# Three row blocks of q's fourth chunk made beside the late query blocks of attention

## The chip, the cores and the metric

The kernel runs on one core of a Trainium2 chip. The metric is the device time of one execution in microseconds; for the kernel before it is the median of three runs. The engines are TensorE (PE, with its weight loads PEld), VectorE (DVE), ScalarE (ACT), GpSimd (POOL) and SyncE (SP), which issues most of the DMAs.

## The reference

Two layers, each an attention block and a Fourier block, on x of 2048 rows and 640 columns:

```python
x = x + _A_ref(_layernorm(x), A_wqkv, A_wo)        # 32 heads of 20 columns
x = x + _B_ref(_layernorm(x), dft_seq_re, dft_seq_im, dft_hid_re, dft_hid_im)
x = x + _A_ref(_layernorm(x), A_wqkv, A_wo)
x = x + _B_ref(_layernorm(x), dft_seq_re, dft_seq_im, dft_hid_re, dft_hid_im)

# _A_ref: q, k, v = x @ wqkv; softmax(q k^T * 20**-0.5) v per head; result @ wo
# _B_ref: real part of DFT over rows of DFT over columns
```

## The kernel before, in words

**Tiling.** 32 heads go in 8 groups of four (`g`), 2048 queries in 4 query blocks of 512 (`qb`), 2048 keys in 16 key chunks of 128 (`kc`). A step `n` is one (`g`, `qb`, `kc`), so a layer's attention has 512 steps, 16 to a query block and 64 to a group (`s.steps`, L461). In each step PE makes four score products (`scores`, L518), two of them side by side on 62 rows each; ACT takes the exponential of two heads at a time (L521), two instructions per step; and PE multiplies the exponentials of an earlier step by v, four heads side by side on 32 columns each (`values`, L529; the trace has eight matmuls per step). Three PSUM buffers hold scores (`p0` to `p2`), seven SBUF buffers exponentials, and one PSUM bank the accumulator of a query block. At a query block's end `finish` divides and transposes on DVE and stores through POOL's queue (L536 to L550).

**The filler.** Only chunk 0 of q and of k (128 of the 640 columns) and half of v are made before attention starts. The rest is made beside it by the generator `work` (L381), piece by piece: k's and q's chunks 1 and 2, the other half of v (16 row tiles), then k's chunk 3, q's chunk 3 ("q's fourth chunk"), k's chunk 4, q's chunk 4. A chunk has four row blocks (`tb`) of 512 rows, each of 15 products of 128 x 128 by 512 columns (L99), cut into pieces of 8 and 7, or in the last two chunks of 5, 5 and 5 (L390). After a row block's last piece `keep` (L194) splits and squares the result on DVE and stores it through POOL's queue; two or four steps later `after` makes the row block's norms with one product (L212) and marks it as made. When the fourth row block of a chunk is done, `after` also splits the next chunk's weights on DVE (L84, L87) and fetches those of the chunk after that through SP's queue.

**What sets the order.** The order on each engine is written out by the loop `sweep` (L553). Per step it calls `begin`, which forces filler that the next heads need (`need`) and works out their softmax shift; loads the next query block's q; issues the two scores; calls `fill`, which issues at most one piece; and then the values that are owed. If a piece was issued, the values of that step are put off. Below step `THIN` = 236 they are made up for at once in the next step, from then on by a step with two steps' values (`calm`, `count = 2`).

`due` (L596) sets the pace of pieces by marks: 16 by step 44, 80 by step 236. From there on pieces come at the steps 2, 7 and 12 of a query block up to step 272 and at 2 and 10 later, until 104 are made.

**Deadlines.** A group's 80 columns of q come from one chunk or two. Group 4 has columns 320 to 399, so it is the first to read chunk 3. Group 6 (columns 480 to 559, `LATE`) is the first to read chunk 4, and is the one group for which only row block 0 of its second chunk has to be made when it starts: for each later query block it asks for the next row block at step 5, works out its own shift (DVE and POOL, L431 to L445; SP's DMA L447 at step 10) and loads q at step 10 (L496 to L499) in place of step 4.

Of the kernel before, what the change touches and what calls it, by code (L numbers as in the profile page):

```python
# [15 lines left out]
S, D, H, DH = 2048, 640, 32, 20  # L16
# [3 lines left out]
ND = D // 128  # L20
NT = S // 128
NB = S // 512
# [1 line left out]
GUARD = 30.0  # L24
NP = NT // 2
NQ = NT // 4
LATE = 512 // (4 * DH)
FIRST = (0, 1, 4, 5)
HD = D // 2
TOL = 2.0 ** -32  # L30
# [5 lines left out]
def mha_fnet_kernel(ctx, tc, x_in, wqk, wv, wo, seq, hid, nat_seq, nat_hid, out):  # L36
# [33 lines left out]
    def bank(tag, shape, name):  # L70
        return pools["pool"].tile(list(shape), F32, name=name, tag=tag)
# [30 lines left out]
    def pieces(blocks, n):  # L102

        todo = [f for b in blocks for f in b]
        for i in range(0, len(todo), n):
            for f in todo[i:i + n]:
                f()
            yield i + n < len(todo)
# [23 lines left out]
    class Qkv:  # L132
# [248 lines left out]
        def work(s):  # L381

            order = [ND + 1, 1, ND + 2, 2, ND + 3, 3, ND + 4, 4]
            w = {0: s.w1}

            def chunk(i):
                c = order[i]
                for tb in range(NB):
                    p = bank("fill", [128, 512], "pqk")
                    for more in pieces([s.product(p, w[i], tb, dc) for dc in range(ND)], 8 if i < 6 else 5):  # L390
                        if more:
                            yield True
                    sq = s.keep(p, c, tb, True, s.fill)

                    def after():
                        s.norms(bank("fill", [H, 512], "pn"), c, tb, sq)
                        s.made.add((c, tb))
                        if tb == NB - 1:
                            s.made.add(c)
                            if i + 1 < len(order):  # L400
                                w[i + 1] = s.weights(s.fill("w", [2, ND, 128], F32R, "wqk"), order[i + 1], True)
                            if i + 2 < len(order):
                                s.fetch(order[i + 2])
                    yield after

            for i in range(4):
                yield from chunk(i)
            for t in range(NT):
                p = bank("fill", [128, HD], "pv")
                for more in pieces([s.value(p, t, dc) for dc in range(ND)], 8):  # L410
                    if more:
                        yield True
                s.own(p, t, 1, True)
                yield None
            s.made.add("v")
            for i in range(4, 8):
                yield from chunk(i)

            s.silent = True
            r = s.bounds()  # L420
            ok = const.tile([128, 1], F32, name="ok", bufs=2)
            V.tensor_scalar(ok[:H], r[:H, 2:3], (GUARD / SCALE) ** 2, None, op0=OP.is_le)

            def after():
                p = bank("fill", [1, 1], "pok")
                PE.matmul(p, ok[:H], one[:H], start=True, stop=True)
                V.tensor_scalar(s.flag, p, float(H), None, op0=OP.is_equal)
            yield after
# [25 lines left out]
    class Attention:  # L454
# [98 lines left out]
        def sweep(s, shift, begin, fill):  # L553
            done = calm = 0
            for n, (g, qb, kc) in enumerate(s.steps):
                begin(n, g, qb, kc)
                last = qb == NB - 1
                if kc == (7 if last else 10 if g == LATE else 4) and not (last and g == H // 4 - 1):
                    s.qload(*((g, qb + 1) if not last else (g + 1, 0)), shift)
                if last and g + 1 < H // 4:  # L560
                    for f, j in {1: [(0, 0)], 9: [(0, 1)], 11: [(1, 0)]}.get(kc, []):
                        s.kload(g + 1, f, j)
                if qb == 0 and kc == 0 and g:
                    s.kload(g, 1, 1)
                s.scores(n, 0)
                s.scores(n, 1)

                more, owed = fill(n) and n >= 2 and n + 1 < len(s.steps), n - 1 - done  # L570
                if n < s.THIN:
                    if more and kc != 1:
                        continue
                    count = owed
                else:
                    if more and owed < 3:
                        calm = n + 2
                        continue
                    count = min(owed, 1)
                    if owed > 1 and (done + 1) % NT and n >= calm:  # L580
                        calm = n + 2
                        count = 2
                for _ in range(count):
                    s.values(done)
                    done += 1
            for n in range(done, len(s.steps)):
                s.values(n)

        def run(s, done, project, check):

            work, tasks, later = s.a.work(), s.a.vweights(1, s.a.fill, pause=[lambda: None] * 2), list(check)
            s.work, s.blocks, s.after, s.rest, s.more, s.landed = True, 0, None, 0, False, 0

            marks = ((0, 0), (44, 16), (s.THIN, 80))

            def due(n):  # L596
                for (n0, k0), (n1, k1) in zip(marks, marks[1:]):
                    if n < n1:
                        return s.blocks < k0 + (k1 - k0) * (n - n0) / (n1 - n0)
                return s.blocks < 80 or s.blocks >= 104 or (n - 1) % NT in ((2, 7, 12) if n < 272 else (2, 10))  # L600

            def block(n):
                try:
                    f = next(work)
                    s.blocks += 1
                    s.more = f is True
                    s.after = (n + (2 if n < s.THIN else 4), f) if f and not s.more else None
                    s.rest = s.after[0] + 2 if s.after else n
                except StopIteration:
                    s.work = False  # L610
                    tasks.extend(done())

            def fill(n):
                if s.after:
                    if n >= s.after[0]:
                        f, s.after = s.after[1], None
                        f()
                elif s.work and n >= s.rest and (s.more and n < s.THIN or due(n + 1)):
                    block(n)
                    s.rest = max(s.rest, n + 2)  # L620
                    return s.work and not s.a.silent

            def compare(n):


                if n < 8:
                    return
                for _ in range(2):
                    if not later or n < s.landed or (len(check) - len(later)) * 490 >= n * len(check):
                        break  # L630
                    task = later.pop(0)
                    if isinstance(task, tuple):
                        s.landed = n + 5
                        task = task[1]
                    task()

            def need(n, *keys):
                while not all(k in s.a.made for k in keys):
                    if s.after:
                        fill(s.after[0])  # L640
                    else:
                        block(n)

            def begin(n, g, qb, kc):


                if qb == NB - 1 and g + 1 < H // 4:
                    when, to = 0, g + 1
                    c0, c1 = to * 80 // 128, ((to + 1) * 80 - 1) // 128
                    keys = [c0, (c1, 0) if to == LATE else c1, ND + c0, ND + c1] + (["v"] if to >= 4 else [])  # L650
                else:
                    when, to, keys = 5, g, [(ND - 1, qb + 1)]
                if to != g or g == LATE and qb < NB - 1:
                    if kc == when:
                        need(n, *keys)
                        s.shift = s.a.bound(to, s.room)
                    if kc - when in (0, 3, 5):
                        next(s.shift)

                if tasks and n % 2 == 0 and n >= 16 and n % 64 < 54:  # L660
                    tasks.pop(0)()
                for f in project.early.get(n, []):
                    f()

            def between(n):
                more = fill(n)
                compare(n)
                return more

            s.sweep("b", begin, between)  # L670
            assert not s.work and not later and not tasks, (len(later), len(tasks))

# [856 lines left out]
```

## Time and profile before

| | us |
|---|---|
| median of 3 runs | 2523.99 (2523.82 to 2524.22) |
| the profiled execution | 2524.65 |
| its span in the trace | 2522.9 |
| attention of layer 1, first exponential to the end of the last | 87.58 to 1123.5 |
| attention of layer 2 | 1337.5 to 2374.6 |

The granted clock of TensorE was 0.999 over the span. In the page's busy digits, PE is at 9 tenths from the second slice to the last but one; ACT is at 8 and 9 in both attention stages and lower in the Fourier stages between and behind them. Filler, row sums of the weight check (L765, L769 on DVE) and the loads of the next stage's weights share the attention stages. Engines other than PE and ACT are busy for less than half of them.

A view of windows is a table by stretches of time: length, then the busy time of each engine with its instructions, the granted clock, the share of the DMA engines and GB/s. A timeline row has the start in us, the time it took, the engine, line, operation, tiles and count; idle time ahead of it, and who ended it, stand in brackets. A group's row has, behind the bar, busy us and mean ns, and behind the second bar idle time of the engine and its releasers.

### The profile page before, as it was taken

Reading aid. Unit: us, or ns where it says so; the run is one execution under the profiler, and the core shown is the slowest. Engines: PE = TensorE matmul, PEld = TensorE weight load, DVE = VectorE, ACT = ScalarE, POOL = GpSimd, SP = SyncE. Lnnn points to the kernel's source line nnn. Section 1 sums busy time; section 2 is a strip of 40 time slices with the busy share of each in tenths; the row PEclk is TensorE's granted clock in tenths of the full one; section 3 lists DMA queues with packets and bytes.
Section 4 is the critical chain, followed back from the end, with each engine's and each line's share of the span. In section 5 each row is a group of like instructions: output and inputs, shape, how many; then the busy total and the mean of one; then the engine's idle time right before and its main releaser. Section 6 shows DMA issues by size and latency. Waiting matters only on the chain. (4 is left out here: it accounts for less than half of the span.)

```text
span 2522.9 us, 43616 instructions
## 1 busy us (share of the span) xinstructions
PE 2492.9 (99%) x16350; PEld 1152.7 (46%) x16350; DVE 976.4 (39%) x2114; ACT 2134.2 (85%) x2430; POOL 520.5 (21%) x1022
## 2 busy tenths in 40 slices
PE   8999999999999999999999999999999999999998
PEld 7644444433333332249885444444433333322596
DVE  6245422243324233426753444223332323332275
ACT  5688899988999999985457888999899999999752
POOL 2012111122111112113321121111221111221133
PEclk9999999999999999999999999999999999999999
DMA  5224221222322223427553332222231222233365
GB/s 187 96 87 126 83 87 43 82 99 80 103 73 88 93 74 113 126 81 245 191 180 99 116 114 85 71 63 71 76 97 52 75 56 68 63 95 105 108 217 194
DMA packets 127024, 262.52 MB, mean 104 GB/s; under 512 B 28736, under 2 KB 53088, under 8 KB 126804
## 3 DMA queue, kind: packets, MB, share of 16 engines
q1 hardware_dynamic: 88212, 159.79, 19.5%
q0 software_dynamic: 38592, 99.85, 12.5%
q8 instruction: 132, 2.16, 0.4%
q14 instruction: 88, 0.72, 0.1%
HBM read 175.29 MB, written 84.21 MB: 103 GB/s over the span
## 5 line engine op out<-in xcount | busy, mean ns | idle before, releaser
L521 ACT ACTIVATE e<-psc 128x1024 f32<-128x1024 f32 x2048 | 1935.9, 1128 | 137.1 <-PE psc L518 103.7
L529 PE MATMUL acc<-e,v 128*32 128x512 f32 x8192 | 1058.6, 602 | 1.9 <-DVE of L536 1.8
L518 PE MATMUL psc<-stq,stk 62*128 62x512 f32 x4096 | 799.3, 458 | 1.3 <-ACT e L521 1.3
L518 PEld LDWEIGHTS psc<-stq,stk 62*128 62x128 f32 x4096 | 339.7, 184 | 808.6 <-ACT e L521 773.5
L529 PEld LDWEIGHTS acc<-e,v 128*32 128x32 f32 x8192 | 188.9, 108 | 370.0 <-issue 344.7
L550 POOL DMA_DIRECT2D o<-oh x256 | 131.7, 523 | 1009.1 <-DVE oh L545 1008.1
L99 PE MATMUL pqk<-xt,wqk 128*128 128x512 f32 x1200 | 318.6, 406 | 3.6 <-DVE wqk L84 1.5
L99 PEld LDWEIGHTS pqk<-xt,wqk 128*128 128x128 f32 x1200 | 213.5, 188 | 92.1 <-issue 41.3
L536 DVE STREAM_TRANSPOSE of<-acc 128x512 f32<-128x512 f32 x64 | 45.9, 717 | 537.1 <-PE acc L529 537.1
L84 DVE CAST hl<-pqk 128x512 fp32r<-128x512 f32 x64 | 44.2, 690 | 432.2 <-PE pqk L99 432.2
L99 PE MATMUL pv<-wv,xt 128*128 128x320 f32 x960 | 159.8, 317 | 0.0
L99 PEld LDWEIGHTS pv<-wv,xt 128*128 128x128 f32 x960 | 141.2, 188 | 25.5 <-issue 21.6
L550 POOL DMA_DIRECT2D o<-ot x256 | 129.0, 512 | 1.9 <-issue 0.7
L207 POOL DMA_DIRECT2D scrq<-hl x40 | 28.4, 709 | 350.9 <-DVE hl L87 219.3
L765 DVE TENSOR_REDUCE far<-cq 128x1 f32<-128x512 f32 (+5 forms) x169 | 98.5, 584 | 5.7
L92 PE MATMUL py<-wo,o 128*128 128x320 f32 x320 | 99.1, 310 | 1.4 <-DVE xr L947 1.4
L93 PE MATMUL py<-wo,o 128*128 128x320 f32 x320 | 98.6, 308 | 0.0
L94 PE MATMUL py<-wo,o 128*128 128x320 f32 x320 | 98.6, 308 | 0.0
L769 DVE TENSOR_TENSOR cq<-cq 128x512 f32<-128x512 f32 (+4 forms) x166 | 96.3, 580 | 2.9 <-DMA cq<-in_nat_seq_dram 2.7
L243 DVE COPY v<-pv 128x320 f32<-128x320 f32 x32 | 15.7, 490 | 204.1 <-PE pv L99 204.1
L207 POOL DMA_DIRECT2D scrk<-hl x40 | 27.9, 697 | 301.4 <-DVE hl L87 252.5
L213 DVE TENSOR_REDUCE top<-pn 32x1 f32<-32x512 f32 x80 | 53.5, 676 | 81.7 <-PE pn L212 81.7
(200 smaller groups left out, 1720.4 us busy)
## 6 DMA issues: line engine op xcount, KB each, us to landing
cq<-in_nat_seq_dram POOLq DMA_DIRECT2D x64, 512.0 KB, 5.5
scrq<-hl POOLq DMA_DIRECT2D x40, 512.0 KB, 3.2
scrk<-hl POOLq DMA_DIRECT2D x40, 512.0 KB, 3.3
stq<-scrq SPq DMA_DIRECT2D x256, 80.0 KB
stk<-scrk SPq DMA_DIRECT2D x128, 160.0 KB
o<-o SPq DMA_DIRECT2D x16, 1280.0 KB
stq<-scrq SPq DMA_DIRECT2D x256, 40.0 KB
stk<-scrk SPq DMA_DIRECT2D x128, 80.0 KB
```

The costliest lines, as they stand in the source:

```text
L92: PE.matmul(out_ap, ah, bh, start=start, stop=False)
L93: PE.matmul(out_ap, ah, bl, start=False, stop=False)
L94: PE.matmul(out_ap, al, bh, start=False, stop=stop)
L99: yield lambda i=i, j=j, k=k: PE.matmul(out_ap, a[i], b[j], start=dc == 0 and k == 0, stop=dc == ND - 1 and k == 2)
L207: G.dma_start(s.scr["qk"[k]][c * 128:(c + 1) * 128, :, tb * 512:(tb + 1) * 512], hl.bitcast(F32))
L213: V.tensor_reduce(s.top[:H, c // ND, c % ND, tb:tb + 1], p, op=OP.max, axis=AX.X)
L518: PE.matmul(p[:, i], s.k[g, kc // 8, j][r, kc % 8 * 128:(kc % 8 + 1) * 128], s.q[g, qb, j][r], start=True, stop=True)
L521: A.activation(e, p, AF.Exp, scale=SCALE)
L529: PE.matmul(s.acc[32 * j:32 * j + 32], s.a.v[kc][:, v0:v0 + 32], s.e[n, j // 2][:, j % 2], start=kc == 0, stop=kc == NT - 1, skip_group_ch ...
L550: G.dma_start(s.o[k, h * DH:(h + 1) * DH, qb * 512:(qb + 1) * 512], hl[k][32 * j:32 * j + DH])
L765: V.tensor_reduce(to, x, op=OP.max, axis=AX.X, apply_absolute_value=True)
L769: V.tensor_tensor(y, x, y, op=op)
```

## The change

`LATE` becomes a pair of groups, 4 and 6. Group 4 now starts when row block 0 of q's chunk 3 is made and asks for the others one by one, as group 6 does for chunk 4. Row blocks 1 to 3 of q's chunk 3 are cut into pieces of five, so that the projection has 107 pieces in place of 104. The mark at step 236 becomes 74 pieces (row block 0 of q's chunk 3 is piece 74), and from there on pieces stand at steps 2, 7 and 12 of each query block until 107 are made.

```diff
-LATE = 512 // (4 * DH)
+LATE = (256 // (4 * DH) + 1, 512 // (4 * DH))
...
-                    for more in pieces([s.product(p, w[i], tb, dc) for dc in range(ND)], 8 if i < 6 else 5):
+                    for more in pieces([s.product(p, w[i], tb, dc) for dc in range(ND)], 8 if (i, tb) < (5, 1) else 5):
...
-                if kc == (7 if last else 10 if g == LATE else 4) and not (last and g == H // 4 - 1):
+                if kc == (7 if last else 10 if g in LATE else 4) and not (last and g == H // 4 - 1):
...
-            marks = ((0, 0), (44, 16), (s.THIN, 80))
+            marks = ((0, 0), (44, 16), (s.THIN, 74))
...
-                return s.blocks < 80 or s.blocks >= 104 or (n - 1) % NT in ((2, 7, 12) if n < 272 else (2, 10))
+                return s.blocks < 74 or s.blocks >= 107 or (n - 1) % NT in (2, 7, 12)
...
-                    keys = [c0, (c1, 0) if to == LATE else c1, ND + c0, ND + c1] + (["v"] if to >= 4 else [])
+                    keys = [c0, (c1, 0) if to in LATE else c1, ND + c0, ND + c1] + (["v"] if to >= 4 else [])
                 else:
-                    when, to, keys = 5, g, [(ND - 1, qb + 1)]
-                if to != g or g == LATE and qb < NB - 1:
+                    when, to, keys = 5, g, [(((g + 1) * 80 - 1) // 128, qb + 1)]
+                if to != g or g in LATE and qb < NB - 1:
```

## The prediction

> **What bounds the kernel now.** I read the page first, for the shares and the costliest groups.
>
> ```profile
> PE 2492.9 (99%) x16350; PEld 1152.7 (46%) x16350; DVE 976.4 (39%) x2114; ACT 2134.2 (85%) x2430; POOL 520.5 (21%) x1022
> ...
> L521 ACT ACTIVATE e<-psc 128x1024 f32<-128x1024 f32 x2048 | 1935.9, 1128 | 137.1 <-PE psc L518 103.7
> ...
> L99 PE MATMUL pqk<-xt,wqk 128*128 128x512 f32 x1200 | 318.6, 406 | 3.6 <-DVE wqk L84 1.5
> ```
>
> A share of 99% says little, because PE is counted busy while it waits with a matmul in flight. The third row says more. L521 is the exponential of attention, two per step (one query block against one key chunk), 16 steps to a query block, 512 to a layer. ACT stood idle 137 us before it, 104 of them for the scores of PE. So somewhere PE is late for ACT. The view of windows, cut at the first exponential of chosen steps, tells where. Its columns are the stretch, its length, the busy time of PE, PEld, DVE, ACT and POOL, the clock and the DMA.
>
> ```profile
> 234.68:617.39 382.71, 380.85 (x2572) 159.88 (x2574) 136.42 (x273) 340.08 (x352) 67.45 (x120) 1.00 0.26 82
> 647.26:677.77 30.51, 30.51 (x212) 10.77 (x215) 9.48 (x17) 30.09 (x34) 4.97 (x9) 1.00 0.19 55
> 677.77:947.34 269.57, 269.57 (x1829) 90.86 (x1828) 92.42 (x203) 267.71 (x289) 52.98 (x96) 1.00 0.27 84
> 1484.80:1868.49 383.69, 381.26 (x2574) 159.89 (x2578) 130.73 (x261) 340.02 (x353) 66.72 (x120) 1.00 0.26 80
> 1928.85:2198.43 269.58, 269.58 (x1829) 90.83 (x1828) 77.45 (x186) 267.70 (x289) 51.18 (x96) 1.00 0.22 65
> ...
> 797.56:827.52 29.96, 29.96 (x207) 10.06 (x203) 10.24 (x18) 29.75 (x33) 6.08 (x11) 1.00 0.26 81
> ```
>
> The first row is steps 64 to 239 of layer 1, the second is steps 256 to 271, the third steps 272 to 415; the fourth and fifth are layer 2's, alike. Early, 11 query blocks take 34.8 us each and ACT works 340 of 383 us. Late, 9 take 29.95 us each and ACT is busy throughout. The groups of ACT in the first and third stretch, with their idle time, confirm it:
>
> ```profile
> L521 ACT ACTIVATE e<-psc 128x1024 f32<-128x1024 f32 x352 | 340.2, 1030 | 42.9 <-PE psc L518 32.7 <-PE acc L529 9.2 <-ACT e L521 0.2
> L521 ACT ACTIVATE e<-psc 128x1024 f32<-128x1024 f32 x289 | 268.8, 1070 | 1.9
> ```
>
> Early, ACT waits 42.9 us for PE: **PE bounds steps up to 236**, where each step also carries filler (projections of q, k, v in pieces). Late it waits 1.9 us: **ACT bounds the late steps**. Moving filler from the first to the second is a trade of PE time that counts for PE time that is partly covered.
>
> **The change, part by part.** (1) Pieces 75 to 80 of the filler, which are row blocks 1 to 3 of q's fourth chunk (45 products, six pieces of 8 or 7), leave the steps before 236 and become nine pieces of 5 after it. The order of instructions of the changed kernel shows that it does this: the rate up to step 236 is 58 pieces in 192 steps for 64, then pieces stand at steps 2, 7 and 12 of each query block through step 412, for two per query block before. The projection ends at nearly the same step (412 for 410).
>
> *What leaves the early steps.* One row block there, from the timeline of PE:
>
> ```profile
> 523.14 0.73 PE L518 MATMUL psc<-stq,stk 62*128 62x512 f32 x4
> ...
> 524.79 0.73 PE L518 MATMUL psc<-stq,stk 62*128 62x512 f32 x4
> 525.45 2.12 PE L99 MATMUL pqk<-xt,wqk 128*128 128x512 f32 x8
> 527.50 0.73 PE L518 MATMUL psc<-stq,stk 62*128 62x512 f32 x4
> ...
> 530.02 0.73 PE L518 MATMUL psc<-stq,stk 62*128 62x512 f32 x4
> 530.68 1.88 PE L99 MATMUL pqk<-xt,wqk 128*128 128x512 f32 x7
> 532.49 0.73 PE L518 MATMUL psc<-stq,stk 62*128 62x512 f32 x4
> ...
> 535.01 0.73 PE L518 MATMUL psc<-stq,stk 62*128 62x512 f32 x4
> ...
> 536.85 0.73 PE L518 MATMUL psc<-stq,stk 62*128 62x512 f32 x4
> ```
>
> Each step starts with four scores, so differences of these starts are step lengths: a plain step 1.65, the 8-piece 2.71, a step that catches up two steps of values 2.52, the 7-piece 2.47, another 2.52, the norm's step 1.84: 13.71 us for six steps. The plain step is 1.66 (657.92 to 659.58 below), six are 9.96. A row block thus costs 3.75 us of PE here, and three of them **11.3 us** per layer.
>
> Not all of it is won. With fewer pieces, stretches of three plain steps come up, and after three of them PE is ahead and waits for ACT. The nearest row is the step at 619.92, after three plain ones:
>
> ```profile
> 619.92 0.89 PE L518 MATMUL psc<-stq,stk 62*128 62x512 f32 x4
> ...
> 622.09 0.73 PE L518 MATMUL psc<-stq,stk 62*128 62x512 f32 x4
> ```
>
> 2.17 us, where the same step without a wait has 2.03 (below): 0.14 us. The order shows some ten such stretches among v's pieces: **1.4 us lost** (0 to 1.8).
>
> *What comes to the late steps.* A piece of five there:
>
> ```profile
> 657.92 0.73 PE L518 MATMUL psc<-stq,stk 62*128 62x512 f32 x4
> ...
> 659.58 0.73 PE L518 MATMUL psc<-stq,stk 62*128 62x512 f32 x4
> 660.24 1.44 PE L99 MATMUL pqk<-xt,wqk 128*128 128x512 f32 x5
> 661.61 0.73 PE L518 MATMUL psc<-stq,stk 62*128 62x512 f32 x4
> ...
> 663.27 0.73 PE L518 MATMUL psc<-stq,stk 62*128 62x512 f32 x4
> ...
> 665.78 0.73 PE L518 MATMUL psc<-stq,stk 62*128 62x512 f32 x4
> ```
>
> The piece's step is 2.03 and its catching up 2.51, so PE needs 10 x 1.66 + 3 x 2.03 + 3 x 2.51 + 0.18 for the norm = 30.40 us for a query block with three pieces, 0.44 over the 29.96 of one with two. The trace has one query block with three, 647.26:677.77 above: 30.51, that is 0.55 more. I take 0.5, between them. Nine query blocks (steps 272 to 415) get a third piece: **4.5 us** (4.0 to 5.0). The cover is PE's waiting for ACT in the two-piece query blocks. With it all gone, a piece costs 2.03 + 2.51 less two steps of 1.66, 1.22 us, and nine 11.0.
>
> (2) *The weights.* A chunk's weights are split on DVE when its predecessor ends. Once in the early steps this comes too late:
>
> ```profile
> 552.29 0.73 PE L518 MATMUL psc<-stq,stk 62*128 62x512 f32 x4
> ...
> 553.78 2.50 PE L99 MATMUL pqk<-xt,wqk 128*128 128x512 f32 x8 [0.75 <-DVE wqk L84]
> ...
> 556.21 0.73 PE L518 MATMUL psc<-stq,stk 62*128 62x512 f32 x4
> ```
>
> 3.92 us for a step of 2.71: 1.2 us. The new order puts three steps between split and use instead of two, so this stall shrinks (0 to 1.2 won, I take 0.6). In exchange the splits for the last two chunks stand two steps ahead of their use, at steps 288 and 352, by this row 0 to 1.2 us each; both come before the query block's own division on DVE, so I take 0.3 for the two. Net **0.3 won** (1.2 won to 2.4 lost).
>
> (3) *Head group 4.* Three more query blocks per layer have their own shift and load q at step 10 instead of 4. Group 6 already does so: SP, then PE.
>
> ```profile
> 901.29 0.25 SPq L447 DMA_DIRECT2D shiftb<-sh  x1
> ...
> 908.10 0.25 SPq L499 DMA_DIRECT2D stq<-shiftb  x1
> ```
> ```profile
> 916.31 0.93 PE L518 MATMUL psc<-stq,stk 62*128 62x512 f32 x4
> ```
>
> The shift waits on SP for DVE; behind it stand the twelve loads, which end their issue at 908.35, 7.96 us before the first scores that read them. PE's sequence runs through, and the third stretch above, which holds two of these turns, costs no more than others: **0**. The shift's power is worked out on POOL, and DVE waits for it with the filler's copies queued behind:
>
> ```profile
> L441 POOL TENSOR_TENSOR bound<-bound,powers 32x1 f32<-32x1 f32 x22 | 14.1, 641 | 96.4 <-DVE bound L435 96.3
> ```
>
> If DVE's idle time did not hide that, it would be 0.64 us for each of the three, 1.9 per layer.
>
> (4) DVE and POOL do the same copies and stores of a row block, later. DVE is idle for two thirds of the late steps, and three more of what eight row blocks already cause there stay under that: 0. Without this cover the norm waits for DVE, as once in the early steps, 0.3 us of the view of waits:
>
> ```profile
> PE pn L212 <- DVE sq L201: 0.3, 1, 0.3
> ```
>
> The tail after step 424 is unchanged.
>
> Sum per layer: -11.3 + 1.4 + 4.5 - 0.3 = -5.7 us; two layers -11.4 us. Against the profiled execution (2524.65 us, span 2522.9) this is 2513.25; against the median of 2523.99, 0.66 below it, **2512.6 us**.
>
> **The rivals.** *The third piece finds no cover.* If two pieces already use up all of PE's slack when every query block has three, each costs 1.22 us: 11.0 in place of 4.5, +6.5 x 2, 2525.6 us: no change. Against it stands the 30.51 of the one such query block; for it, that this one came after a lighter one and could draw on scores made ahead.
>
> *The early steps are not PE's.* If ACT or a chain through both set the early pace, nothing is saved and only the late cost stays: +4.5 x 2, 2533.0 us. It decides wherever the removed 11.3 us shrinks below 5.6. Against it stand the 42.9 us for which ACT waited on PE.
> The Trainium skill (Perfetto Trace Analysis, Identifying the Most-Contended Engine) judges TensorE's headroom by the busy share of its weight loads, not of its matmuls. By that the 159.88 of 382.71 us make PE far from bound and ACT, at 340, the contended engine, which would be this rival; the trace here disagrees, since ACT's idle time has PE as its releaser.
>
> *Late q loads (the slower side).* In group 4 the loads land after the first scores that need them, on three turns a layer, six in all. They must land 7.96 us after issue before it costs anything, and 11.4 / 6 = 1.9 us more before the kernel is slower. The trace has no landing of these loads; the nearest are
>
> ```profile
> cq<-in_nat_seq_dram POOLq DMA_DIRECT2D x64, 512.0 KB, 5.5
> scrq<-hl POOLq DMA_DIRECT2D x40, 512.0 KB, 3.2
> ```
>
> both shorter for larger transfers. At 3.8 us of waiting per turn: 2535.4 us.
>
> That the pieces do not move as said is excluded by the order of instructions.
>
> **How the numbers follow.** Forecast 0.84, no cover 0.07, early steps not PE's 0.05, late loads 0.04. The bounds of the unknown terms: at best 11.3 + 1.2 - 4.0 = 8.5 per layer, 2507; at worst 11.3 - 1.8 - 2.4 - 5.0 = 2.1, 2519.8. The range is 2507 to 2519.5; beyond it lie the three rivals. A measurement of this kernel tells about 0.2% (5 us) from no change, so faster means under 2518.9: 0.82, the forecast less 0.02 for its worst corner. Within 0.2%: that 0.02 and the first rival, 0.09. Slower: the other two, 0.09.
>
> **What would show it.** Right: query blocks of steps 272 to 415 near 30.45 us each, the steps up to 240 shorter by about 10 us in a layer, ACT idle some 10 us less there. Wrong: late query blocks near 31.2 (no cover), early steps as long as before, waits of L518 for a DMA at the turns of steps 272, 288 and 304, or waits for wqk at steps 290 and 354.

## The result and the profile after

| | before | after |
|---|---|---|
| median of 5 runs each, us | 2523.82 (2523.25 to 2524.22) | 2512.00 (2511.89 to 2512.25) |
| span of the profiled execution, us | 2522.9 | 2510.1 |
| attention of layer 1, from the first turn to the last, us | 997.48 | 991.64 |
| attention of layer 2, us | 998.67 | 991.94 |

The change takes 11.8 us off. The ratio is 0.9953, 95% interval 0.9942 to 0.9964. The forecast was 2512.6, the range 2507 to 2519.5. A turn is here the transposition of a query block's accumulator on DVE (L536); between the profiled executions attention lost 5.84 and 6.73 us, 12.6 of the 12.7 us that the span lost.

First the page of after: its engines and two of its groups.

```profile
PE 2479.9 (99%) x16350; PEld 1147.5 (46%) x16350; DVE 980.2 (39%) x2144; ACT 2133.1 (85%) x2430; POOL 524.1 (21%) x1028
...
L521 ACT ACTIVATE e<-psc 128x1024 f32<-128x1024 f32 x2048 | 1934.4, 1121 | 126.0 <-PE psc L518 94.1
L529 PE MATMUL acc<-e,v 128*32 128x512 f32 x8192 | 1057.9, 602 | 3.9 <-DVE of L536 3.8
```

PE has exactly as many matmuls as before (16350), and ACT as many instructions; what fell by 11.1 us is ACT's idle time ahead of the exponentials (137.1 before), 9.6 of it waiting for scores. The second group is the surprise: values now wait 3.8 us for DVE's transposition. In the page of before it was 1.8 us:

```profile
L529 PE MATMUL acc<-e,v 128*32 128x512 f32 x8192 | 1058.6, 602 | 1.9 <-DVE of L536 1.8
```

The view of windows of after shows where the time went, with the stretches of before cut at the same steps (layer 1: 64 to 239, 256 to 271, 272 to 415; layer 2: 64 to 239, 272 to 415; last, the query block of steps 336 to 351, as in the prediction's last row).

```profile
234.34:607.14 372.80, 371.01 (x2524) 151.85 (x2526) 127.20 (x259) 337.22 (x352) 65.29 (x117) 1.00 0.25 79
637.02:667.52 30.50, 30.50 (x212) 10.81 (x215) 10.21 (x22) 30.09 (x34) 5.54 (x10) 1.00 0.17 54
667.52:941.15 273.63, 273.63 (x1876) 96.60 (x1875) 100.92 (x220) 269.73 (x290) 56.13 (x101) 1.00 0.28 89
1478.58:1851.03 372.45, 370.65 (x2524) 151.71 (x2526) 121.79 (x246) 337.26 (x352) 64.52 (x117) 1.00 0.25 77
1911.41:2185.06 273.65, 273.65 (x1876) 96.52 (x1875) 85.96 (x203) 269.72 (x289) 54.29 (x101) 1.00 0.24 70
789.13:819.52 30.39, 30.39 (x212) 10.71 (x211) 10.25 (x18) 29.96 (x33) 6.15 (x11) 1.00 0.25 80
```

The early stretch fell from 382.71 to 372.80, 9.9 us. The late one rose from 269.57 to 273.63, 4.1 us, and 48 or 47 matmuls came into it (1829 to 1876) as they left the early one. The query block with three pieces that both kernels have stayed at 30.5. For layer 2 the row of before in the prediction begins 0.46 us ahead of step 64's first exponential; cut at the exponential it is

```profile
1485.26:1868.49 383.23, 380.80 (x2572) 159.76 (x2574) 130.53 (x260) 339.85 (x352) 66.72 (x120) 1.00 0.26 80
```

so layer 2 lost 10.8 early and rose by 4.1 late. The groups of ACT in after's first and third stretch say the same from the other side: early it waits 35.9 us (42.9 before), late 3.9 (1.9 before).

```profile
L521 ACT ACTIVATE e<-psc 128x1024 f32<-128x1024 f32 x352 | 337.3, 1036 | 35.9 <-PE psc L518 28.6 <-PE acc L529 6.5
L521 ACT ACTIVATE e<-psc 128x1024 f32<-128x1024 f32 x290 | 271.7, 1043 | 3.9
```

### The profile page after: what moved, and what is told of

It reads as the page before. It is cut to its first block, busy times and chain, and to the rows that moved or that the text cites. A ratio compares the mean times of both kernels' runs of the same rounds, so it can differ in the third digit from the quotient of the medians.

```text
span 2510.1 us, 43669 instructions
## 1 busy us (share of the span) xinstructions
PE 2479.9 (99%) x16350; PEld 1147.5 (46%) x16350; DVE 980.2 (39%) x2144; ACT 2133.1 (85%) x2430; POOL 524.1 (21%) x1028
## 3 DMA queue, kind: packets, MB, share of 16 engines
q0 software_dynamic: 38592, 99.85, 12.6%
## 5 line engine op out<-in xcount | busy, mean ns | idle before, releaser
L518 PE MATMUL psc<-stq,stk 62*128 62x512 f32 x4096 | 786.2, 455 | 1.3 <-ACT e L521 1.3
L518 PEld LDWEIGHTS psc<-stq,stk 62*128 62x128 f32 x4096 | 335.5, 184 | 792.3 <-ACT e L521 762.6
L536 DVE STREAM_TRANSPOSE of<-acc 128x512 f32<-128x512 f32 x64 | 45.8, 716 | 349.9 <-PE acc L529 349.3
```

The source lines that it names most:

```text
L518: PE.matmul(p[:, i], s.k[g, kc // 8, j][r, kc % 8 * 128:(kc % 8 + 1) * 128], s.q[g, qb, j][r], start=True, stop=True)
```

## The experiments

**The theory** (trade): 11.3 us of PE's time per layer leave steps in which every microsecond of PE lengthens the kernel and go to steps in which PE waits for ACT, so that only a part of it shows. **The rivals**: the gain is the vanished stalls and the new order, not the work (order); it is the cut into smaller pieces (cutting); the late pieces cost their whole 1.22 us and the gain comes from elsewhere (no cover), or they are free; the late loads of group 4 cost or hide something. Two more theories came up as experiments failed: that the late slack needs **evenly spaced** pieces, and that a row block which ends at a turn delays the **hand-over** of the accumulator. Each run is compared with the kernel before on the same chip, whose medians were 2523.67 to 2523.89.

**e1_left_out: the late work taken away**, from the changed kernel. One product of fifteen is left of each of the three row blocks.

```diff
-                    for more in pieces([s.product(p, w[i], tb, dc) for dc in range(ND)], 8 if (i, tb) < (5, 1) else 5):
+                    blocks = [s.product(p, w[i], tb, dc) for dc in range(ND)]
+                    if i == 5 and tb:
+                        blocks = [[lambda: PE.matmul(p, w[i][:, 0, 0], s.xt[tb, 0][0], start=True, stop=True)]]
+                    for more in pieces(blocks, 8 if (i, tb) < (5, 1) else 5):
...
-                return s.blocks < 74 or s.blocks >= 107 or (n - 1) % NT in (2, 7, 12)
+                return s.blocks < 74 or s.blocks >= 101 or (n - 1) % NT in ((2, 7, 12) if n < 320 else (2, 10))
```

> The changed kernel with row blocks 1 to 3 of q's fourth chunk left out but for one product of fifteen each (that part of q is not computed); splits, stores and norms stay, the pace of the late pieces is three per query block up to step 320 and two from there on. It shows the early saving almost alone. Trade theory (11.3 us of TensorE time per layer leave the early steps, some 1.4 us come back as waits, each third late piece costs 0.45): early -9.9 per layer as in the changed kernel, three query blocks with a third piece +1.3, step 240 to 255 some 0.4 shorter: -9.0 x 2 against the kernel before, 2505.8 us (2504.5 to 2507.5), about 6 us under the changed kernel. Stall theory (the gain is the 1.2 us wait for weights at step 212 that is gone, and the slower pace): as fast as the changed kernel less what the late pieces cost, and the early steps as long as there. If late pieces were free: 2512 again, less 0.8.

Measured: 2505.94 us (2505.60 to 2506.42). Its windows of the early and the late stretch of layer 1 (like those of e2_made_twice, e3_uncut and e10_bunched below, they are cut at the first scores of a step, 0.6 to 1.1 us ahead of its first exponential):

```profile
233.49:605.95 372.46, 370.26 (x2518) 151.30 (x2514) 128.67 (x261) 336.62 (x353) 65.77 (x119) 1.00 0.26 81
666.26:937.05 270.79, 270.79 (x1846) 92.82 (x1843) 95.39 (x214) 268.27 (x289) 54.61 (x99) 1.00 0.28 86
```

The early stretch is as in after; the late one is 2.8 us shorter. So the late pieces do cost: 6.1 us in both layers together. "Free" falls.

**e2_made_twice: the late work added, nothing taken away**, from the kernel before. The three row blocks are made early as before; behind them, among the late steps, come as many products again, in pieces of five, with the next chunk's weights and a result that nobody reads.

```diff
+                for tb in range(1, NB) if i == 5 else ():
+                    p = bank("fill", [128, 512], "pqk")
+                    for more in pieces([s.product(p, w[6], tb, dc) for dc in range(ND)], 5):
+                        yield True if more else None
...
-                return s.blocks < 80 or s.blocks >= 104 or (n - 1) % NT in ((2, 7, 12) if n < 272 else (2, 10))
+                return s.blocks < 80 or s.blocks >= 113 or (n - 1) % NT in (2, 7, 12)
```

> The kernel before with the cost of the late pieces alone: everything is made early as before, and nine further pieces of five products, whose result nobody reads, are put among the late steps at the changed kernel's pace (no copies, stores or norms for them). Trade theory: nine third pieces at 0.45 less the three norms that are missing (0.18 each), 3.5 to 4.1 us per layer: 2531.3 us (2530 to 2532.5). No cover: nine at 1.22 us, 11 us per layer: 2546. Late pieces free: 2523.8.

Measured: 2532.57 us (2532.43 to 2532.71), 8.9 above before and 0.07 above the upper end of what was expected. Early and late stretch:

```profile
233.54:616.02 382.48, 380.62 (x2571) 159.76 (x2568) 136.73 (x274) 339.63 (x353) 67.22 (x121) 1.00 0.26 82
676.84:950.01 273.17, 273.17 (x1869) 95.84 (x1865) 94.11 (x201) 269.51 (x289) 54.27 (x98) 1.00 0.27 86
```

The early stretch is that of before (382.71), the late one nearly that of after: the two halves of the trade stand each by itself. Nine pieces of five per layer would have cost 22 us in both layers without cover. "No cover" falls.

**e6_pace: the new places alone**, from the kernel before: pieces of 8 and 7 and of 5 as before, but at 2, 7 and 12 throughout.

```diff
-                return s.blocks < 80 or s.blocks >= 104 or (n - 1) % NT in ((2, 7, 12) if n < 272 else (2, 10))
+                return s.blocks < 80 or s.blocks >= 104 or (n - 1) % NT in (2, 7, 12)
```

> The kernel before with the late pace alone: its 24 late pieces come at three per query block instead of two and are done at about step 360; nothing leaves the early steps. Trade theory: the query blocks with three pieces cost 30.41 instead of 29.96, and those that become empty 29.25 instead of 29.96. Of nine query blocks (steps 272 to 415) six get a third piece, +2.7, and three become empty, -2.1: +0.6 per layer, 2525.0 us (2523.5 to 2526). If the three-per-query-block pace were itself the gain: under 2520.

Measured: 2526.51 us (2526.07 to 2526.89), 2.8 us above before and 0.5 above the range expected: a miss in size. Attention rose by 0.68 and 1.27 us. The denser pace is a small loss by itself, so the new places of the late pieces are not the source of the gain. What is left of "order" is the stall on the weights, which is worth 1.2 us per layer (below), a fifth of the gain.

**e5_group5: one more group that asks late**, from the changed kernel: group 5 too works out its own shifts and loads q at step 10.

```diff
-LATE = (256 // (4 * DH) + 1, 512 // (4 * DH))
+LATE = (256 // (4 * DH) + 1, 256 // (4 * DH) + 2, 512 // (4 * DH))
```

> The changed kernel with the late shift and the late loads of q (step 10 instead of 4) for head group 5 as well, which needs neither: three more such turns per layer, six in all, and no filler moved. Trade theory: the loads have 8 us to spare and the shift is hidden, 0: 2512.0 us (2511.6 to 2512.5). Late-load theory: the three turns of group 4 already cost something, and so would these, 1 us of waiting for scores on each of them making 6 us: 2515 or more.

Measured: 2512.42 us (2511.89 to 2513.05), the same as after. Late loads cost nothing measurable, in group 5 as in group 4.

**e3_uncut: the change without the cut**, pieces of 8 and 7 for the three row blocks.

```diff
-                    for more in pieces([s.product(p, w[i], tb, dc) for dc in range(ND)], 8 if (i, tb) < (5, 1) else 5):
+                    for more in pieces([s.product(p, w[i], tb, dc) for dc in range(ND)], 8 if i < 6 else 5):
...
-                return s.blocks < 74 or s.blocks >= 107 or (n - 1) % NT in (2, 7, 12)
+                return s.blocks < 74 or s.blocks >= 104 or (n - 1) % NT in (2, 7, 12)
```

> The changed kernel with row blocks 1 to 3 of q's fourth chunk in pieces of 8 and 7 instead of three of five, moved out of the early steps all the same. Trade theory: TensorE's products are what counts, not how they are cut; the query blocks from step 240 to 303 then sum to 120.6 us by the step lengths (2.71, 2.47, 2.03, 2.51, 1.66) for 121.2 in the changed kernel, with 0.7 more in the query block before them: 2512.2 us (2511 to 2514). If the finer cut carries the gain: towards 2520 or more. If a piece of 8 starves ScalarE beyond the sum of steps, by the 0.7 us gaps seen behind such pieces early: six pieces, up to 4 us per layer, 2520.

Measured: 2516.75 us (2516.52 to 2518.16), a miss: 4.75 us, two fifths of the gain, are gone. The windows of the query blocks at steps 240 and 256:

```profile
607.06:638.19 31.13, 31.13 (x212) 10.80 (x208) 11.08 (x21) 29.98 (x33) 6.26 (x11) 1.00 0.38 111
638.19:669.31 31.12, 31.12 (x212) 10.97 (x208) 11.98 (x25) 29.97 (x33) 5.37 (x10) 1.00 0.20 60
```

Two pieces of 8 and 7 are as many products as three of 5, and the steps add up to 30.3 us, yet the query block takes 31.1. Between two pieces there are more plain steps (steps without a piece) in a row. That gave the theory of even spacing: the three score buffers hold the scores of one and a half steps, so PE gets only so far ahead of ACT. In a plain step it gains some 0.17 us on ACT (1.66 us against 1.83); after about three of them the buffers are full, and what it could save beyond that it waits away.

**e10_bunched: the same pieces, unevenly spaced**, from the changed kernel, made to test that.

```diff
-                return s.blocks < 74 or s.blocks >= 107 or (n - 1) % NT in (2, 7, 12)
+                return s.blocks < 74 or s.blocks >= 107 or (n - 1) % NT in (2, 5, 8)
```

> The changed kernel with the late pieces at steps 2, 5 and 8 of a query block instead of 2, 7 and 12: the same work, bunched. Sum theory as predicted (a query block with three pieces costs TensorE's 30.40 us wherever they stand): 2512 to 2513. Evenness theory (three score buffers let TensorE run ahead by three plain steps, then each further one waits 0.15 us for ScalarE; the uncut pieces cost 31.13 us a query block by it, where their steps sum to 30.3): seven plain steps in a row, four or five of them waiting, 31.1 us a query block and eleven query blocks a layer: +7 to 8 per layer, 2527 us (2522 to 2530), and all of the gain is lost.

Measured: 2527.92 us (2527.77 to 2528.13), 15.9 above after and 4.0 above before. Windows of steps 272 to 415 and of one query block of them:

```profile
667.85:947.69 279.84, 279.84 (x1877) 97.81 (x1874) 101.77 (x224) 271.25 (x289) 56.40 (x101) 1.00 0.28 89
698.96:730.06 31.10, 31.10 (x214) 10.86 (x210) 10.86 (x25) 30.23 (x33) 7.38 (x13) 1.00 0.31 94
```

No matmul more, 6.2 us longer; 31.10 per query block for after's 30.40. The timeline of PE at the starts of six steps in the long plain run shows how:

```profile
724.90 0.73 PE L518 MATMUL psc<-stq,stk 62*128 62x512 f32 x4
...
726.56 0.73 PE L518 MATMUL psc<-stq,stk 62*128 62x512 f32 x4
...
728.22 0.86 PE L518 MATMUL psc<-stq,stk 62*128 62x512 f32 x4
...
730.00 0.98 PE L518 MATMUL psc<-stq,stk 62*128 62x512 f32 x4
...
731.91 0.84 PE L518 MATMUL psc<-stq,stk 62*128 62x512 f32 x4
...
733.67 0.91 PE L518 MATMUL psc<-stq,stk 62*128 62x512 f32 x4
```

The step lengths are 1.66, 1.66, 1.78, 1.91, 1.76. Ahead of these stand one more plain step and the norm's step. So after three plain steps the four scores take 0.84 to 0.98 us instead of 0.73, and the steps lengthen to about ACT's pace, 1.83 us (a query block without filler takes 29.33 us, turn to turn). What ends the wait is an exponential, which frees a score buffer for the next weight load of the scores:

```profile
730.41 0.26 PEld L518 LDWEIGHTS psc<-stq,stk 62*128 62x128 f32 x2 [0.23 <-ACT e L521]
```

What PE waits here it lacks at the next piece. The cover is whole only where a piece comes after at most three plain steps.

**e4_one_block: a third of the change.** Only row block 3 moves.

```diff
-                    for more in pieces([s.product(p, w[i], tb, dc) for dc in range(ND)], 8 if (i, tb) < (5, 1) else 5):
+                    for more in pieces([s.product(p, w[i], tb, dc) for dc in range(ND)], 8 if (i, tb) < (5, 3) else 5):
...
-            marks = ((0, 0), (44, 16), (s.THIN, 74))
+            marks = ((0, 0), (44, 16), (s.THIN, 78))
...
-                return s.blocks < 74 or s.blocks >= 107 or (n - 1) % NT in (2, 7, 12)
+                return s.blocks < 78 or s.blocks >= 105 or (n - 1) % NT in ((2, 7, 12) if n < 320 else (2, 10))
```

> A third of the dose: only row block 3 of q's fourth chunk is moved behind step 236 (mark 78 pieces, three per query block up to step 320, two from there on). Trade theory: early -3.75 per layer and some 0.5 of waits back, three third pieces +1.35, so -1.9 per layer, 2520.0 us (2518.5 to 2522); in proportion to the full change. Stall theory: all of the gain or none of it, according to whether the weights' split stands clear of its use: 2512 to 2514, or 2523.8.

Measured: 2524.68 us (2523.04 to 2526.13), a miss: no gain at all. The profiled execution, at 2523.04 us, was its fastest; attention in it is 997.82 us in each layer, 0.5 us less than before for both together, where 3.8 were expected. PE's work moved as priced, 3.76 us less early per layer, and steps 242 to 417 rose by 1.3 us. The view of PE's waits, steps 98 to 241 of layer 1 and of layer 2, has the reason:

```profile
PE acc L529 <- DVE of L536: 3.1, 5, 2.4
...
PE acc L529 <- DVE of L536: 2.1, 5, 1.1
```

Its columns are total, count and the longest. One wait of 2.4 us; the timeline around it, DVE and PE:

```profile
581.60 1.88 PE L99 MATMUL pqk<-xt,wqk 128*128 128x512 f32 x7
...
583.52 0.69 DVE L84 CAST hl<-pqk 128x512 fp32r<-128x512 f32 x1 [8.21 <-PE pqk L99]
...
584.24 0.69 DVE L87 TENSOR_TENSOR hl<-pqk,hl 128x512 fp32r<-128x512 f32 x1
...
584.85 0.68 DVE L201 TENSOR_TENSOR sq<-hl 128x512 bf16<-128x512 f32 x1
...
585.45 0.68 DVE L769 TENSOR_TENSOR cq<-cq 128x512 f32<-128x512 f32 x1
586.16 0.69 DVE L765 TENSOR_REDUCE far<-cq 128x1 f32<-128x512 f32 x1
586.77 0.70 DVE L536 STREAM_TRANSPOSE of<-acc 128x512 f32<-128x512 f32 x1
...
587.53 1.06 PE L529 MATMUL acc<-e,v 128*32 128x512 f32 x8 [2.39 <-DVE of L536]
```

The last piece of a row block falls into step 225, just at the turn. DVE stands idle 8.2 us, then does the row block's three operations and two of the weight check ahead of the transposition that frees the accumulator, and PE waits. So the work moved as meant, but another piece came into a bad slot by it.

**e8_one_block_clear: no piece at any turn**, from e4_one_block.

```diff
-                elif s.work and n >= s.rest and (s.more and n < s.THIN or due(n + 1)):
+                elif s.work and n >= s.rest and (n >= s.THIN or n % NT not in (0, 1)) and (s.more and n < s.THIN or due(n + 1)):
```

> The run that moved one row block gained nothing, and its trace shows TensorE waiting 2.4 us at step 226 of layer 1 and 1.1 us in layer 2 for the transpose of the accumulator, which stood on VectorE behind a row block's three copies and a weight check; the row block had ended at step 1 of the query block. This is that kernel with no piece issued at steps 0 and 1 of a query block below step 236. Hand-over theory (a row block that ends at the turn delays the accumulator's transpose, and the trade itself is as priced): the wait goes and the third of the gain appears, 2520.0 us (2518.5 to 2521.5). If the trade is not in proportion (one block simply brings nothing): 2523.5 to 2525.

Measured: 2524.92 us (2523.38 to 2526.48), a miss. The wait at step 226 went, but the edit shifts pieces in every query block. By the waits of PE in steps 28 to 62 of layer 1, one new wait took its place,

```profile
PE pn L212 <- DVE sq L201: 2.1, 1, 2.1
```

a norm forced at once where pieces now crowd, with the same 2.1 us in layer 2; some 5 us of PE's work came from ahead of step 98 to behind it; and the span ended 9.2 us after the last operation of DVE, for 6.8 in e4_one_block. It moved too much to decide.

**e12_one_block_225: that one slot alone**, from e4_one_block.

```diff
-                elif s.work and n >= s.rest and (s.more and n < s.THIN or due(n + 1)):
+                elif s.work and n >= s.rest and n not in (224, 225) and (s.more and n < s.THIN or due(n + 1)):
```

> The run that moved one row block, with one edit: no piece at steps 224 and 225, so the row block that ended at step 225 ends at step 226, behind the turn, and all pieces from step 236 on stand as they were. (Keeping steps 0 and 1 clear everywhere took that wait away, but pushed pieces together at step 48, where a forced norm waited 2.4 us for VectorE, and the time did not fall.) Hand-over theory: the waits of 2.4 us in layer 1 and 1.1 us in layer 2 go, up to 0.3 us of the shorter kind stays in each, and the trade of one row block, -3.76 early and +1.33 late per layer, comes out: 3 us under the run without the edit, 2521.6 us (2520.5 to 2522.5). If one row block simply brings nothing: 2524.7.

Measured: 2521.50 us (2520.42 to 2522.73), as expected, 3.2 us under e4_one_block. The waits of PE over the same steps, layer 1 and layer 2:

```profile
PE acc L529 <- DVE of L536: 0.7, 4, 0.2
...
PE acc L529 <- DVE of L536: 1.0, 4, 0.5
```

Turn to turn, the query block of steps 208 to 223 fell from 40.26 to 36.23 us in layer 1, and the piece that was barred lengthened the next one from 31.96 to 33.76. The hand-over theory holds: the time came back with this one slot. Against before, the gain of a third of the work is 2.3 us in the medians, and 3.8 us, 1.9 per layer, in the attention of the profiled executions.

**e9_checks_clear: the weight check off the turns**, from the changed kernel, which has a small wait of this kind:

```diff
-                if n < 8:
+                if n < 8 or n % NT in (0, 1):
```

> The changed kernel with no weight checks issued on VectorE at steps 0 and 1 of a query block; they are made up for in the steps behind. Its trace has one long wait for the accumulator's transpose, 0.76 us at step 226 of layer 1, with a check of 1.4 us between the row block's copies and the transpose. Hand-over theory: that wait goes, 0.5 us of 0.76, and nothing else moves: 2511.5 us (2510.8 to 2512.3).

Measured: **2511.24 us** (2511.08 to 2511.78), ratio to before 0.9949, interval 0.9935 to 0.9963. It is the fastest version, 0.8 us under the change, and within what was expected. The timeline of after at step 226, and then that of this kernel:

```profile
576.71 0.69 DVE L769 TENSOR_TENSOR cq<-cq 128x512 f32<-128x512 f32 x1
577.43 0.69 DVE L765 TENSOR_REDUCE far<-cq 128x1 f32<-128x512 f32 x1
578.03 0.70 DVE L536 STREAM_TRANSPOSE of<-acc 128x512 f32<-128x512 f32 x1
...
578.79 1.06 PE L529 MATMUL acc<-e,v 128*32 128x512 f32 x8 [0.56 <-DVE of L536]
```
```profile
576.25 0.68 DVE L201 TENSOR_TENSOR sq<-hl 128x512 bf16<-128x512 f32 x1
...
577.46 0.72 DVE L536 STREAM_TRANSPOSE of<-acc 128x512 f32<-128x512 f32 x1 [0.53 <-PE acc L529]
...
578.23 1.07 PE L529 MATMUL acc<-e,v 128*32 128x512 f32 x8
```

Without the two check operations DVE waits for PE there, not PE for DVE. Attention fell by 0.6 and 1.4 us. The 0.6 is this wait. Layer 2 has none at step 226; there the gain comes from two waits of 0.56 us at steps 34 and 82, which went as well. The kernel before has these two too, so this part is an improvement of its own and takes nothing back that the change cost. The profiled spans differ by less than 0.2 us, because 1.0 us more passed behind DVE's last operation (last section) and 0.7 us more between the two attention stages.

**e7_aligned: the pieces of steps 96 to 236 at 2, 7 and 12 of their query blocks too**, from the changed kernel, so that no row block ends at a turn.

```diff
-                        return s.blocks < k0 + (k1 - k0) * (n - n0) / (n1 - n0)
+                        return s.blocks < k0 + (k1 - k0) * (n - n0) / (n1 - n0) + (3 if n >= 96 else 0) and (n < 96 or (n - 1) % NT in (2, 7, 12))
```

> The changed kernel with the pieces of the early steps from 96 on put at fixed steps of the query block (2, 7, 12 and two steps behind each) instead of by the mark alone. The changed kernel's trace has two residual waits of TensorE early: 0.24 us at step 2 of a query block when its first values wait for the transpose of the accumulator, and 0.12 to 0.19 us after three plain steps. A piece at step 2 puts the values off and the first wait goes; long plain stretches between pieces bring more of the second. By counts of steps some 2.4 us per layer less and up to 1.5 us more: 2510.2 us (2508 to 2512.5). If the position of pieces does not matter early: 2512.0.

Measured: 2512.02 us (2511.72 to 2513.13), no difference. The waits for the transposition are gone from those steps, but attention is 990.75 and 992.07 us for 991.64 and 991.94. By step lengths, the fixed places leave stretches of more than three plain steps, and PE waits at their ends, at steps 153 to 156, 174 to 178, 202 to 204, 218 to 220 and 234 to 236: 0.11 to 0.24 us a step, some 2.9 us per layer. That took the place of the waits that went. The expected 1.8 us were not there.

**e11_v_cut: v's row tiles in pieces of five products in place of eight**, from the changed kernel, to get rid of its stretches of three plain steps.

```diff
-                for more in pieces([s.value(p, t, dc) for dc in range(ND)], 8):
+                for more in pieces([s.value(p, t, dc) for dc in range(ND)], 5):
...
-            marks = ((0, 0), (44, 16), (s.THIN, 74))
+            marks = ((0, 0), (44, 16), (96, 32), (203, 80), (s.THIN, 90))
...
-                return s.blocks < 74 or s.blocks >= 107 or (n - 1) % NT in (2, 7, 12)
+                return s.blocks < 90 or s.blocks >= 123 or (n - 1) % NT in (2, 7, 12)
```

> An attempt at a faster kernel: the changed kernel with v's pieces too cut into five products (three per row tile instead of 8 and 7), spread evenly over steps 96 to 203. By the evenness theory the waits of 0.12 to 0.19 us behind three plain steps go, ten per layer, and TensorE's sum stays: some 1.4 us per layer less the waits that new positions bring, 2510.5 us (2509 to 2512.5). If the early steps are at TensorE's sum in any case: 2512.0.

Measured: 2515.88 us (2515.24 to 2517.30), a miss, 3.9 above after. Attention rose by 0.55 and 0.97 us; a row of PE's waits in steps 27 to 246 of layer 1 names the new one,

```profile
PE acc L529 <- DVE of L536: 2.0, 5, 0.9
```

with its longest at step 114, where more and smaller pieces bring DVE's copies to a turn. Of the rest, 2.4 us lie behind DVE's last operation, at the end of the program (last section).

## Why the prediction was right, point by point

To compare the terms, steps without a wait were priced from the timelines: four scores 0.80 us, eight values 0.86, a product of q or k 0.239, of v 0.155, the norm 0.18. What a stretch is longer than the sum of its steps is PE's waiting. Per layer, layer 1 / layer 2:

| | before | after |
|---|---|---|
| steps 98 to 241, sum of work | 306.4 | 295.1 |
| steps 98 to 241, waiting | 2.0 / 1.9 | 3.5 / 2.4 |
| steps 242 to 417, sum of work | 321.2 | 332.5 |
| steps 242 to 417, waiting (layer 1) | 8.8 | 1.7 |

**The mechanism held.** 11.3 us of PE's work went from the first stretch to the second, where 7.1 us of waiting disappeared under it. e1_left_out and e2_made_twice show the two halves apart.

- *What leaves the early steps*, 11.3 forecast: 11.29.
- *Waits after three plain steps*, 1.4 lost: ten waits of 0.12 to 0.19 us, 1.45 in layer 1, and some 1.2 in layer 2. After's timeline at one of them, step 130, from its scores to the next step's, is 2.19 us for 2.04 without a wait:

```profile
375.25 0.89 PE L518 MATMUL psc<-stq,stk 62*128 62x512 f32 x4
376.07 1.43 PE L99 MATMUL pv<-wv,xt 128*128 128x320 f32 x8
377.44 0.73 PE L518 MATMUL psc<-stq,stk 62*128 62x512 f32 x4
```

- *What comes late*, 4.5 (4.0 to 5.0): 4.06 and 4.07, nine times 0.45. The prediction chose 0.5 between the sum of steps (30.40) and the one measured query block (30.51). The sum was the better of the two: nine query blocks in 273.63 us are 30.40 each, the length of PE's work, so PE sets it and waits no more. The 30.51 of the block of steps 256 to 271 was no better row: by step lengths PE still waits 0.35 us at its step 256 and 0.19 at 258, in both kernels, since no piece stands between steps 247 and 258.
- *The weights*, 0.3 won: 1.2 won. The views of waits of the early steps, before and then after:

```profile
PE pqk L99 <- DVE wqk L84: 0.8, 1, 0.8
...
PE acc L529 <- DVE of L536: 0.4, 2, 0.2
...
```
```profile
PE acc L529 <- DVE of L536: 1.4, 6, 0.6
...
```

  The stall at step 212 is gone whole, and no wait stands at steps 290 or 354: the two steps ahead of these uses were enough.
- *Group 4's loads*, 0: 0, by e5_group5.
- **Missed:** the last view's first row. With the pieces of the early steps at other places, values wait longer for the transposition, 1.4 us for 0.4 (layer 2: 1.4 for 0.9). One of the new waits, 0.56 us in layer 1 alone, stands at step 226, where a row block ends near the turn; e9_checks_clear takes it away. Three more in each layer are of 0.17 or 0.18 us, at steps 146, 194 and 210, where no piece puts off the first values of a query block; e7_aligned, with a piece at that place, has none of them. The prediction costed DVE's copies only for the norm, not for the transposition queued behind them.
- **ACT's idle time**, a sign that was to show it: "some 10 us less" in the steps up to 240. It fell by 7.0 us in layer 1 (42.9 to 35.9), while the stretch became 9.9 us shorter; the rest is 2.9 us by which ACT's busy time in it fell.

So the sum was -5.7 per layer and came out at -5.8 and -6.7. The errors partly offset each other: late pieces 0.4 cheaper, weights 0.9 better, hand-over 0.5 to 1.0 worse. That the forecast came within 0.6 us of the median is therefore in part luck; the direction and the size of the two large terms are not.

Two things the prediction had without naming them. Its late price holds only because the pieces stand five steps apart (e3_uncut, e10_bunched); the same 11.3 us bunched would have made the kernel slower than before. And its early price holds only where no turn is hit: e4_one_block moved a third of the work and won nothing. The Trainium skill (Perfetto Trace Analysis, Optimization Strategy) says that a gap which repeats on the engine that should be saturated can mean too few buffers for the next tile. The waits of 0.12 to 0.19 us after each third plain step, with three score buffers, agree with that; no run here changed the number of buffers.

Of the rivals, "no cover" would have had late query blocks near 31.2 and they took 30.40; "early steps not PE's" would have left 382.7 us and it was 372.8, which also speaks against the headroom by weight loads that the prediction set beside it; "late loads" has no wait of L518 for a DMA. The late waits that remain (1.7 us) are for the most part not in the query blocks that got a third piece: 1.0 us stands at steps 242, 254, 255, 256 and 258, each behind three or more plain steps, and is the same in the kernel before.

## What to carry to other kernels

Before you move work out of a stretch that an engine bounds, price both places by the waiting of that engine: here 63% of the moved time (7.1 of 11.3 us) was hidden where PE had been waiting for ACT. Slack of an engine that runs ahead through a few buffers cannot be saved up: cut and space the moved work so that a piece comes before the buffers are full. Then look which engine's queue the moved or re-spaced pieces now cross at a hand-over; one bad slot (2.4 us in layer 1, 1.1 in layer 2) ate nearly all of what a third of this change brings.

## What the runs showed of the hardware that was not expected

The end of the program differs between the profiled executions, though its code does not. From the end of DVE's last operation to the end of the span it is 6.9 us in the kernel before, 7.6 in after, 6.8 in e4_one_block, 8.6 in e9_checks_clear, 9.2 in e8_one_block_clear and 10.1 in e11_v_cut. The last row of the chain of waits of after, whose span is 2510.1, is the first below; of e11_v_cut, the span and that row, the second:

```profile
2502.11 0.40 DVE xd L1241
```
```profile
span 2514.3 us, 43671 instructions
...
2503.84 0.40 DVE xd L1241
```

In that time the traces show the last output's DMA and fetches of instructions, and no engine's work. So differences of 1 to 3 us between two orders of the same work need not lie in the order; what sets the end was not found, and with one profiled execution of each kernel it is open whether the end goes with the kernel or differs from execution to execution. Runs of one kernel also spread by different amounts: 3.1 us in 10 and 11 runs of e4_one_block and e8_one_block_clear, 0.4 in five of the changed kernel, and in the kernel before 1.0 in five runs and 2.8 in 21; that too stays open.
